# Expert rows kept as two 16-bit planes and turned by a transposing DMA, in a fused attention and expert kernel

## The chip, the cores and the metric

One core of a Trainium2 chip runs the whole program. The metric is the device time of one execution in microseconds; the kernel before takes 730.2 us (median of three runs, 729.65 to 731.32).

## The reference, cut to what matters

Three stages follow each other. The first is bucketed attention over 2 batches, 8 heads, 768 positions and 64 numbers per head; its result is laid out as 1536 token rows of 512 numbers. The second gives each token to the one expert of eight with the largest gate logit. The third is a gated feed-forward over all tokens.

```python
x = attn_out.transpose(0, 2, 1, 3).reshape(B * S, H * D)      # 1536 x 512
e_idx = np.argmax(x @ w_gate, axis=1)
for e in range(8):
    mask = e_idx == e
    h = np.maximum(x[mask] @ w1[e], 0.0)                       # 512 -> 1024
    out[mask] = gate_w[mask, None] * eom[mask, e, None] * (h @ w2[e])
return ((out @ w_a) * (out @ w_b)) @ w_out                     # 512 -> 1536 -> 512
```

## The kernel before, in words

All arithmetic is float32, most of it as a rounded high part and a rest (names ending in h and l), with three matmuls for one product. The order of every engine's instructions is the order of the program text, since a manual schedule is switched on.

**Attention.** A loop over 96 steps (16 heads of 6 query tiles, `h` and `t`) issues the scores of the next tile, the row minimum and the scale (`smax`, lines 164 and 165, on DVE), the exponential (line 173, on ACT), six TensorE transposes (line 186) and their copies out, and the product with v. Two heads later `o_out` (line 229) multiplies by an identity beside the gate weights; DVE writes the logits (line 248) and the head's 64 columns of `x_all` (line 249), and POOL adds the logits (line 251). POOL also makes the low parts of q and k (lines 116 to 119).

**Routing and scatter.** When batch 0 is done, `router` computes each token's slot, and `scat` sends each block of 128 rows of `x_all` by an indirect DMA from POOL to its rows in the DRAM table `xr`: 224 rows for each expert. Between two scatters POOL writes one column, `spare` (line 427). Batch 1's six scatters run after attention (259 to 267 us). For expert 0, `x0_load` fetches the rows of batch 0, and `x0_first`, `x0_hot` and `x0_add` put batch 1's rows in by matmuls, so that expert 0 can start ahead of the scatters.

**Experts.** A loop over 64 steps (expert `e`, slice `f` of 128 hidden columns). Each step issues `mm1(e, f)` (12 matmuls of 224 columns, lines 930 to 932), then `mm2` of the step before (8 matmuls, lines 970 and 971), then the split of the weights of coming steps (`w_split`: ACT line 484, DVE line 485), each of which issues the load of a slice four steps on (`w_load`, line 475, SP's queue). `x_load(e)` (line 910, SP's queue, ahead of the weight loads that follow it in the text) fetches an expert's rows, 2 times 128 rows of 2 KB. It waits for all scatters. `x_tpose` (line 912), at two steps of the expert before, turns half of them by four TensorE transposes (line 921); ACT and DVE split the result out of PSUM (lines 924 and 925). At the stage's start POOL clears `y_h`, `y_l` and `y_w` by twelve writes (line 815); `y_store(0)` writes into them at step (1, 1).

**Third stage.** A hand-made order of side work (`todo_of`) is laid between the matmuls.

Of the kernel before, what the change touches and what calls it, by code (L numbers as in the profile page):

```python
# [20 lines left out]
S, D, NB, NH = 768, 64, 2, 8  # L21
NT = 6
N, DM, E, FF, F2 = 1536, 512, 8, 1024, 1536
C = 224
# [9 lines left out]
def attn_moe_kernel(ctx: ExitStack, tc: tile.TileContext, xin, cst, projd, wblk, wmoe, w2in, out):  # L34
# [19 lines left out]

    xr = dram.tile([E * C + N, DM], F32, name="xr")
    idtab = dram.tile([N, 2], F32, name="idtab")
# [15 lines left out]
    noff_i = const.tile([128, 24], I32, name="noff_i")  # L72
    x_all = big.tile([128, 12, DM], F32, name="x_all")
    sums = big.tile([128, 96, 2], F32, name="sums")
# [131 lines left out]
    def av_group(h, q, ks):  # L206
# [3 lines left out]
        for k in ks:  # L210
# [3 lines left out]
            )  # L214

    oT, rs = {}, {}

# [11 lines left out]
    def o_out(h, q=None):  # L229
        b, hh = divmod(h, NH)  # L230
        o, r = oT.pop((h, q)), rs.pop((h, q))
        p = ps_m.tile([128, 512], F32, tag="m", name="m")
        t0, nt = q or (0, NT)
        t = slice(b * 6 + t0, b * 6 + t0 + nt)
        lp = sm.tile([128, nt, 16], F32, tag=f"lp{nt}", name="lp", bufs=2) if hh else lg[:, t]
        xo = x_all[:, t, hh * 64:(hh + 1) * 64]
# [12 lines left out]
        DVE.tensor_tensor(out=xo, in0=ps[..., :64], in1=rr.to_broadcast(sh + [64]), op=ALU.mult)  # L249
        if hh:  # L250
            (DVE if hh >= NH - 2 else POOL).tensor_tensor(out=lg[:, t], in0=lg[:, t], in1=lp, op=ALU.add)

    def router(gi):
# [103 lines left out]
        def scat(k):  # L357
            return lambda: scatter(
                scat_x, out=xr, out_offset=bass.IndirectOffsetOnAxis(ap=pos_i[:, k:k + 1], axis=0), in_=x_all[:, k],
                in_offset=None,  # L360
            )
# [8 lines left out]
    def x_split(d, t0=6, n=6):  # L370
        if d not in XH:
            XH[d] = [tb.tile([128, 6, 128], F32R, tag="tb"[i] + "qk"[d % 2], name="xh") for i in range(2)]
        h, l = (a[:, t0 - 6:t0 - 6 + n] for a in XH[d])
        x = x_all[:, t0:t0 + n, d * 128:(d + 1) * 128]
# [5 lines left out]
    def x0_load():  # L380
        x0["g"] = xp.tile([128, 2, DM], F32, tag="x", name="x0")
        for c in range(2):
            after(nc.sync.dma_start(out=x0["g"][:, c], in_=xr[c * 128:(c + 1) * 128]), scat_x)

# [40 lines left out]
    def scatter(done, **kw):  # L425
        if done:
            POOL.memset(spare, 0.0)
        ins = POOL.indirect_dma_start(**kw).ins
        for other in done:
            tc.declare_no_dep(ins, other, reason="each scatter writes rows of its own")  # L430
        done.append(ins)

    def after(ins, done):
        ins = ins.ins
        for other in done:
            tc.add_manual_dep(ins, other.name, dep, reason="reads what all the scatters wrote")
# [99 lines left out]
    def chunk(e, col, rr, new, psum):  # L536
# [11 lines left out]
        DVE.tensor_copy(tf[:, 0:1], tk.bitcast(I32)[:, 0:1])  # L548
        DVE.tensor_scalar(out=xi, in0=tf[:, 0:1], scalar1=float(E * C), scalar2=None, op0=ALU.add)
        x = new("f_x", [128, DM])  # L550
        POOL.indirect_dma_start(out=x, out_offset=None, in_=xr, in_offset=bass.IndirectOffsetOnAxis(ap=xi, axis=0))
        DVE.tensor_tensor(out=tf[:, 1:2], in0=rr, in1=col[:, 0:1], op=ALU.is_ge)
# [49 lines left out]
    with tc.manual_schedule():  # L602
# [49 lines left out]
        def set_up(k):  # L652
# [11 lines left out]
            elif k == 5:  # L664
# [10 lines left out]
        L = NHD - 1  # L675
        acts = (x0_load, lambda: x_split(0), lambda: (w_split(0, 0, POOL), w_split(0, 1, POOL)), lambda: x_split(1), lambda: x_split(2),
                lambda: w_split(1, 0, POOL))
# [5 lines left out]
        for g in range(NG):  # L683
# [8 lines left out]
            if 2 * NT <= g < 2 * NT + (E * C + N) // 256:  # L692
                for i in (g - 2 * NT,):
                    nc.sync.dma_start(
                        out=xr[i * 256:(i + 1) * 256].rearrange("(p r) d -> p r d", p=128),
                        in_=zeros[0].unsqueeze(1).to_broadcast([128, 2, 512]),
                    )
# [61 lines left out]
            if h and h < L and t == 5 and K["avl"].count(5):  # L759
                o_evac(h - 1)  # L760
            side(2)
            for f in extra.get((h - L + 1, t), ()):
                f()
# [15 lines left out]
        x0_hot(POOL, 7)  # L779
        x0_hot(POOL, 8)  # L780
        for t in (6, 7, 8):
            x0_add(t)
# [4 lines left out]
        rb["s2p"]()  # L787
        x_split(3, 10, 2)
        x0_add(9)
        for t in (10, 11):  # L790
# [21 lines left out]
        y_w = yp.tile([128, 4, N + C], F32, name="y_w")  # L812
        for y in (y_h.bitcast(F32), y_l.bitcast(F32), y_w):
            for d in range(4):
                POOL.memset(y[:, d], 0.0)
        r2 = ctx_2.enter_context(tc.tile_pool(name="r2", bufs=2, reuse_waits="tile"))
# [6 lines left out]
        yt = ctx_m.enter_context(tc.tile_pool(name="yt", bufs=4, reuse_waits="tile"))  # L823
        px = ctx_m.enter_context(tc.tile_pool(name="px", bufs=1, space=PSUM, reuse_waits="tile"))
        py = ctx_m.enter_context(tc.tile_pool(name="py", bufs=5, space=PSUM, reuse_waits="tile"))
# [78 lines left out]
        XG, HT, Y = {}, {}, {}  # L904

        def x_load(e):
            XG[e] = [xg.tile([128, DM], F32, tag=f"xg{c}", name=f"xg{c}") for c in range(2)]
            for c in range(2):
                r = e * C + c * 128
                after(nc.sync.dma_start(out=XG[e][c], in_=xr[r:r + 128]), scat_x)  # L910

        def x_tpose(e, halves):
            if e not in XS:
                XS[e] = [xs.tile([128, 4, C], F32R, tag="x" + "hl"[i], name="x" + "hl"[i]) for i in range(2)]
            h, l = XS[e]
            p = {i: px.tile([128, 512], F32, tag="x", name="xt") for i in halves}
            for c in range(2):
                for i in halves:
                    for j in range(2):
                        d, o = 2 * i + j, j * 256 + c * 128  # L920
                        PE.transpose(p[i][:, o:o + 128], XG[e][c][:, d * 128:(d + 1) * 128], ident)
            for i in halves:
                src = p[i].rearrange("p (a b) -> p a b", a=2)[:, :, :C]
                ACT.activation(h[:, 2 * i:2 * i + 2], src, ACTF.Copy)
                DVE.tensor_tensor(
                    out=l[:, 2 * i:2 * i + 2], in0=src, in1=h.bitcast(F32)[:, 2 * i:2 * i + 2], op=ALU.subtract
                )

# [102 lines left out]
        for n, (e, f) in enumerate(steps):  # L1031
# [212 lines left out]
        def todo_of(c, f):  # L1244
# [7 lines left out]
            def put(k, g, *a):  # L1252
                m[k].append(lambda: g(*a))
# [11 lines left out]
            elif (c, f) == (1, 0):  # L1265
                conv(1, 2, 0, 1, 1, 2)
                for k, g in ((0, t[7]), (1, t[8]), (2, t[9]), (3, t[10]), (4, t[11]), (5, u[1])):
                    put(k, g)
                put(3, w2_c, 1)
                for k, nm in ((4, "22"), (5, "s4"), (6, "21")):  # L1270
                    put(k, part, 1, nm)
                put(6, cc_work)
            elif (c, f) == (0, 1):
                for k, g in ((1, u[2]), (2, u[3]), (5, u[4]), (6, u[6])):
                    put(k, g)
# [10 lines left out]
            elif c == 0:  # L1286
# [131 lines left out]
```

## Time and profile before

| what | value |
|---|---|
| median of three runs | 730.2 us |
| the profiled execution, its own time | 730.29 us |
| span in its profile | 728.5 us |
| TensorE clock granted, mean | 0.997 |
| busy PE / DVE / ACT / POOL | 98% / 76% / 61% / 32% of the span |
| attention and its tail | 0 to 260 us |
| experts | 260 to about 430 us |
| third stage | to the end |

Starts and lengths are in microseconds from the span's start. PE is the matmuls, PEld the weight loads that overlap them. The time of the execution is 1.8 us above its span: what lies around the span.

### The profile page before, as it was taken

How to read it: one execution, taken by the hardware profiler on the slowest of the kernel's cores; microseconds unless marked ns; L12 is line 12 of the kernel's file. 1: busy time of each engine (PE TensorE's matmuls, PEld its weight loads, DVE VectorE, ACT ScalarE, POOL GpSimd, SP SyncE). 2: the span in 40 equal slices, each digit the busy share in tenths (PEclk: the TensorE clock that was granted, in tenths of full speed). 3: DMA queues.
4: the chain of work that ended last, by engine and by line, in shares of the span. 5: the costliest groups of instructions: out<-in, count | busy, mean ns of one | idle time of the engine just before them, and what ended most of it. 6: DMA issues, size and time to landing. Idle time of an engine off the chain costs nothing.

```text
span 728.5 us, 13206 instructions
## 1 busy us (share of the span) xinstructions
PE 711.2 (98%) x4561; PEld 609.0 (84%) x4562; DVE 552.4 (76%) x1102; ACT 448.0 (61%) x962; POOL 233.6 (32%) x269
## 2 busy tenths in 40 slices
PE   8899999999999999999999999999999999999995
PEld 6566776676676689999999999889999999999994
DVE  6778877888786778778778778886887877777644
ACT  5887787777777547667778766566443453444320
POOL 4232333232633368112220003234222333223234
PEclk9999999999999999999999999999999999999998
DMA  6357351131311048778798641132111222122013
GB/s 229 133 187 277 114 178 59 59 116 61 113 38 63 15 141 281 218 194 237 230 271 253 211 128 58 31 115 86 59 58 59 87 65 81 46 71 59 1 57 120
DMA packets 42681, 88.48 MB, mean 121 GB/s; under 512 B 7328, under 2 KB 10736, under 8 KB 42608
## 3 DMA queue, kind: packets, MB, share of 16 engines
q1 hardware_dynamic: 39936, 81.07, 36.0%
q0 software_dynamic: 2304, 6.31, 2.3%
q8 instruction: 38, 0.62, 0.4%
q14 instruction: 35, 0.29, 0.1%
q10 hardware_dynamic: 368, 0.20, 0.1%
HBM read 73.32 MB, written 13.12 MB: 119 GB/s over the span
## 4 chain that ended last, share of the span: by engine, by line
PE 82%; DVE 5%; issue 5%; ACT 4%; POOL 2%; DMA 1%; ACTq 0%; DVEq 0%; POOLq 0%; SPq 0%
PE tp L186 9%; PE av L201 8%; PE y L970 6%; PE s L158 4%; PE s L159 4%; PE h L932 4%; PE h L931 4%; PE h L930 4%; PE y L971 3%; PE abb L1186 3%; PE aba L1186 3%; PE abb L1188 3%; PE abb L1187 3%; PE aba L1188 3%; PE aba L1187 3%
## 5 line engine op out<-in xcount | busy, mean ns | idle before, releaser
L164 DVE TENSOR_REDUCE mm<-s 128x1 f32<-128x768 f32 x96 | 91.0, 948 | 25.2 <-PE s L159 24.5
L173 ACT ACTIVATE p<-s,sb 128x768 f32<-128x768 f32 x96 | 94.8, 988 | 22.3 <-DVE sb L165 21.7
L186 PEld LDWEIGHTS tp<-cs,p 128*128 128x128 f32 x576 | 64.2, 140 | 36.9 <-ACT p L173 23.5
L186 PE MATMUL tp<-cs,p 128*128 128x128 f32 x576 | 82.1, 278 | 4.9 <-ACT p L173 4.1
L485 DVE TENSOR_TENSOR wl<-wr,wh 128x512 fp32r<-128x512 f32 x125 | 81.4, 692 | 7.2 <-ACT wh L484 0.8
L190 ACT ACTIVATE pt<-tp 128x384 f32<-128x384 f32 x143 | 64.9, 487 | 32.6 <-PE tp L186 32.6
L901 POOL TENSOR_TENSOR pc<-t,pc 128x256 fp32r<-128x256 f32 x38 | 32.3, 854 | 156.5 <-ACT pc L900 141.9
L970 PE MATMUL y<-hl,wh 128*128 128x448 f32 x224 | 74.8, 377 | 0.4 <-DVE hl L944 0.3
L484 ACT ACTIVATE wh<-wr 128x512 fp32r<-128x512 f32 x128 | 73.5, 623 | 1.8 <-DMA wr<-wmoe 1.7
L158 PE MATMUL s<-tk,tq 76*128 76x384 f32 x192 | 73.0, 380 | 0.3 <-DVE tq L135 0.3
L930 PE MATMUL h<-xh,wh 128*128 128x224 f32 x256 | 71.4, 279 | 0.2 <-ACT xh L418 0.2
L931 PE MATMUL h<-xl,wh 128*128 128x224 f32 x256 | 70.2, 274 | 0.3 <-DVE xl L419 0.3
L932 PE MATMUL h<-xh,wl 128*128 128x224 f32 x256 | 70.4, 275 | 0.0
L201 PE MATMUL av<-pt,v 128*64 128x384 f32 x360 | 68.0, 499 | 0.2 <-DVE r L225 0.2
L159 PE MATMUL s<-bk,bq 128*128 128x384 f32 x192 | 65.1, 339 | 0.0
L971 PE MATMUL y<-hl,wl 128*128 128x224 f32 x224 | 59.5, 266 | 0.0
L1076 ACT ACTIVATE gh<-p 128x384 fp32r<-128x384 f32 x21 | 11.0, 526 | 64.4 <-DVE p L1205 64.4
L930 PEld LDWEIGHTS h<-xh,wh 128*128 128x128 f32 x256 | 48.9, 191 | 1.2 <-ACT xh L418 0.4
L931 PEld LDWEIGHTS h<-xl,wh 128*128 128x128 f32 x256 | 49.1, 192 | 0.5 <-DVE xl L419 0.5
L201 PEld LDWEIGHTS av<-pt,v 128*64 128x64 f32 x360 | 21.9, 136 | 32.8 <-issue 24.5
L932 PEld LDWEIGHTS h<-xh,wl 128*128 128x128 f32 x256 | 49.1, 192 | 0.0
L851 ACT ACTIVATE x<-r 128x512 uint8<-128x512 uint8 x36 | 28.5, 791 | 33.2 <-DVE x L848 33.2
(258 smaller groups left out, 1940.6 us busy)
## 6 DMA issues: line engine op xcount, KB each, us to landing
wr<-wmoe SPq DMA_DIRECT2D x128, 256.0 KB
r<-w2in SPq DMA_DIRECT2D x36, 512.0 KB
x<-xin SPq DMA_DIRECT2D x30, 384.0 KB
xr<-zero SPq DMA_DIRECT2D x13, 512.0 KB
xg<-xr SPq DMA_DIRECT2D x14, 256.0 KB
v<-xin SPq DMA_DIRECT2D x16, 192.0 KB
wb<-wblk SPq DMA_DIRECT2D x1, 640.0 KB
x<-xin SPq DMA_DIRECT2D x3, 192.0 KB
```

The lines of the kernel that those rows point to most:

```text
L158: PE.matmul(p[:, c, :384], T[h, 0][:76, qs], T[h, 1][:76, sl], start=True, stop=False)
L159: PE.matmul(p[:, c, :384], B[h, 0][:, qs], B[h, 1][:, sl], start=False, stop=True)
L164: DVE.tensor_reduce(out=m[:, 1:2], in_=st[g][:, :, :384], axis=AX.XY, op=ALU.min)
L173: ACT.activation(p.rearrange("p (c n) -> p c n", c=2), st.pop(g)[:, :, :384], ACTF.Exp, scale=scl.pop(g), bias=nbs.pop(g), accum_out=sums[ ...
L186: PE.transpose(ps[:, j * 128:(j + 1) * 128], pt_[g][:, k * 128:(k + 1) * 128], ident)
L201: PE.matmul(av[h][c * 64:(c + 1) * 64, :384], v, PT[h][:, k, c * 384:(c + 1) * 384], start=(k == 0), stop=(k == NT - 1), skip_group_check= ...
L485: eng.tensor_tensor(out=l, in0=r, in1=h.bitcast(F32), op=ALU.subtract)
L930: PE.matmul(ps, wh, xh, start=first, stop=False)
L931: PE.matmul(ps, wh, xl, start=False, stop=False)
L932: PE.matmul(ps, wl, xh, start=False, stop=last)
L970: PE.matmul(p, wh[:, w], hl, start=(f == 0), stop=False, skip_group_check=True)
L971: PE.matmul(p[:, 0], wl[:, w], hl[:, 0], start=False, stop=(f == 7), skip_group_check=True)
```

## The change

`xr` becomes a table of 32-bit words whose rows hold two planes: 512 low halves of the float32 numbers, then 512 high halves, each of 16 bits. Batch 0's heads go through a small tile `xf`, and POOL writes their halves into `x_q` (`to_planes`); batch 1's stay as float32 in `x_b` for the matmuls of expert 0, and POOL writes their halves later (`late_planes`). `x_load` becomes one DMA that turns 224 rows of 1024 16-bit numbers into eight blocks of 128 partitions; POOL joins the halves (`x_join`), and ACT and DVE split them from SBUF (`x_parts`). The TensorE transposes of experts 1 to 7 and their PSUM bank are gone. The column write between scatters becomes a no-operation. Eight of the twelve clearing writes move behind expert 1's join, and a few pieces of side work of the third stage change their slots.

```diff
+    def halves(ap):
+        return ap.bitcast(U16).rearrange("p t (n a) -> p t a n", a=2)
+    def to_planes(t0, nt, hh, src):
+        o = x_q.bitcast(U16).rearrange("p t (a n) -> p t a n", a=2)[:, t0:t0 + nt, :, hh * 64:(hh + 1) * 64]
+        POOL.tensor_copy(o, src)
+    def late_planes(hh, t0=0, nt=6):
+        to_planes(t0, nt, hh, halves(x_b)[:, t0:t0 + nt, :, hh * 64:(hh + 1) * 64])
...
         if hh:
             (DVE if hh >= NH - 2 else POOL).tensor_tensor(out=lg[:, t], in0=lg[:, t], in1=lp, op=ALU.add)
+        if not b:
+            to_planes(0, 6, hh, halves(xf))
+        elif NH + 3 <= h < L:
+            late_planes(hh)
...
+    def x0_join():
         x0["g"] = xp.tile([128, 2, DM], F32, tag="x", name="x0")
+        q = x0.pop("q").bitcast(U16).rearrange("p c (a n) -> p c a n", a=2)
         for c in range(2):
-            after(nc.sync.dma_start(out=x0["g"][:, c], in_=xr[c * 128:(c + 1) * 128]), scat_x)
+            POOL.tensor_copy(halves(x0["g"])[:, c], q[:, c])
...
-            POOL.memset(spare, 0.0)
+            POOL.nop()
...
+            if h == L - 2 and t > 2:
+                late_planes(t - 3)
...
         x0_hot(POOL, 8)
+        late_planes(NH - 1, 0, 4)
...
         x_split(3, 10, 2)
+        late_planes(NH - 1, 4, 2)
...
+        y_clear(y_h.bitcast(F32))
...
         def x_load(e):
-            XG[e] = [xg.tile([128, DM], F32, tag=f"xg{c}", name=f"xg{c}") for c in range(2)]
-            for c in range(2):
-                r = e * C + c * 128
-                after(nc.sync.dma_start(out=XG[e][c], in_=xr[r:r + 128]), scat_x)
+            XG[e] = xg.tile([128, 8, C], U16, tag="xg", name="xg")
+            after(nc.sync.dma_start(out=XG[e], in_=x_rows[e * C:(e + 1) * C], transpose=True), scat_x)
+        def x_join(e):
+            XI[e] = xg.tile([128, 4, C], F32, tag="xi", name="xi", bufs=1)
+            POOL.tensor_copy(
+                XI[e].bitcast(U16).rearrange("p d (n a) -> p a d n", a=2), XG.pop(e).rearrange("p (a d) n -> p a d n", a=2)
+            )
+        def x_parts(e, i):
+            h, l = (x[:, 2 * i:2 * i + 2] for x in XS[e])
+            src = XI[e][:, 2 * i:2 * i + 2]
+            ACT.activation(h, src, ACTF.Copy)
+            DVE.tensor_tensor(out=l, in0=src, in1=h.bitcast(F32), op=ALU.subtract)
...
-            if f in (5 if e == 0 else 4, 6) and e + 1 < E:
-                x_tpose(e + 1, (f // 2 - 2,))
+            if e + 1 < E:
+                if f == (3 if e else 5):
+                    x_join(e + 1)
+                for i in range(2):
+                    if f == ((4, 6) if e else (6, 7))[i]:
+                        x_parts(e + 1, i)
+            if (e, f) == (0, 5):
+                y_clear(y_l.bitcast(F32), y_w)
...
-                put(6, cc_work)
-                for k, g in ((1, u[2]), (2, u[3]), (5, u[4]), (6, u[6])):
+                for k, g in ((0, u[1]), (1, u[2]), (2, u[3]), (4, cc_work), (5, u[4]), (6, u[6])):
...
-                    for k, at in ((0, 4), (1, 4), (2, 5)):
+                    for k, at in ((0, 3), (1, 6), (2, 6)) if f == 2 else ((0, 4), (1, 4), (2, 5)):
```

## Rows read from the trace of the kernel before

**Rows 1.** Page, span and busy time of each engine.

```profile
span 728.5 us, 13206 instructions
PE 711.2 (98%) x4561; PEld 609.0 (84%) x4562; DVE 552.4 (76%) x1102; ACT 448.0 (61%) x962; POOL 233.6 (32%) x269
```

**Rows 2.** Stretches of the expert stage: busy of each engine, clock, DMA share, GB/s.

```profile
269.00:281.00 12.00, 11.67 (x88) 11.19 (x89) 10.11 (x31) 7.95 (x20) 12.00 (x8) 1.00 0.86 279
281.00:302.00 21.00, 21.00 (x162) 20.41 (x161) 17.33 (x41) 15.30 (x38) 9.33 (x10) 1.00 0.79 232
```

**Rows 3.** Groups by line, the transposes of expert rows and their split.

```profile
L921 PE MATMUL xt<-cs,xg 128*128 128x128 f32 x56 | 8.4, 273 | 0.0
...
L925 DVE TENSOR_TENSOR xl<-xt,xh 128x448 fp32r<-128x448 f32 x14 | 8.7, 622 | 0.6
...
L924 ACT ACTIVATE xh<-xt 128x448 fp32r<-128x448 f32 x14 | 7.6, 543 | 3.2 <-PE xt L921 3.2
```

**Rows 4.** Timeline of PE: first matmul of four steps, one transpose group (start, length).

```profile
276.54 0.35 PE L930 MATMUL h<-xh,wh 128*128 128x224 f32 x1
...
279.23 0.60 PE L921 MATMUL xt<-cs,xg 128*128 128x128 f32 x4
279.58 0.35 PE L930 MATMUL h<-xh,wh 128*128 128x224 f32 x1
...
282.27 0.28 PE L930 MATMUL h<-xh,wh 128*128 128x224 f32 x1
...
284.88 0.28 PE L930 MATMUL h<-xh,wh 128*128 128x224 f32 x1
```

**Rows 5.** Timeline of SP's queue, then ACT, then DVE, 268 to 277 us.

```profile
268.96 0.80 SPq L910 DMA_DIRECT2D xg<-xr  x2
269.87 11.43 SPq L475 DMA_DIRECT2D wr<-wmoe  x14
...
274.73 1.30 ACT L484 ACTIVATE wh<-wr 128x512 fp32r<-128x512 f32 x2 [1.72 <-DMA wr<-wmoe]
...
275.39 1.36 DVE L485 TENSOR_TENSOR wl<-wr,wh 128x512 fp32r<-128x512 f32 x2 [0.85 <-ACT wh L484]
```

**Rows 6.** Page, DMA queues: packets, MB, share of 16 engines' span.

```profile
q1 hardware_dynamic: 39936, 81.07, 36.0%
...
q10 hardware_dynamic: 368, 0.20, 0.1%
```

**Rows 7.** Timeline of DVE in step (0, 7), and PE in the step after.

```profile
281.59 0.39 DVE L944 SCALAR_TENSOR_TENSOR hl<-h,hl 128x224 fp32r<-128x224 f32 x1
282.11 1.29 DVE L485 TENSOR_TENSOR wl<-wr,wh 128x512 fp32r<-128x512 f32 x2
...
283.05 0.27 PE L931 MATMUL h<-xl,wh 128*128 128x224 f32 x1
```

**Rows 8.** Timeline of all engines in one attention head, 80 to 85 us.

```profile
80.17 0.82 POOL L119 CAST bk<-tk 64x768 fp32r<-64x768 f32 x1
80.44 0.56 DVE L165 SCALAR_TENSOR_TENSOR sb<-mm 128x2 f32<-128x2 f32 x1
...
81.31 0.39 POOL L251 TENSOR_TENSOR lg<-lg,lp 128x96 f32<-128x96 f32 x1 [0.33 <-DVE lp L248]
...
82.70 0.16 DVE L165 SCALAR_TENSOR_TENSOR sb<-mm 128x2 f32<-128x2 f32 x1
...
82.98 0.99 ACT L173 ACTIVATE p<-s,sb 128x768 f32<-128x768 f32 x1 [0.54 <-DVE sb L165]
...
84.23 0.74 PEld L186 LDWEIGHTS tp<-cs,p 128*128 128x128 f32 x6
```

**Rows 9.** Timeline of POOL: tail of attention, between two scatters, clearing writes.

```profile
255.38 0.73 POOL L376 TENSOR_TENSOR xh<-x_all,xh 128x256 fp32r<-128x256 f32 x1 [0.37 <-ACT xh L375]
...
260.57 0.12 POOL L427 MEMSET spare<- 128x1 f32 x1
...
281.08 6.11 POOL L815 MEMSET y_w<- 128x1760 f32 x4
```

More of the change, by code (lines that the diff above doesn't have):

```diff
@@ L12 @@
 U32 = mybir.dt.uint32
+U16 = mybir.dt.uint16
 U8 = mybir.dt.uint8
@@ L53, in attn_moe_kernel @@
     ident = cs[:, C_ID:C_ID + 128]
-    xr = dram.tile([E * C + N, DM], F32, name="xr")
+    xr = dram.tile([E * C + N, DM], U32, name="xr")
     idtab = dram.tile([N, 2], F32, name="idtab")
@@ L72, in attn_moe_kernel @@
     noff_i = const.tile([128, 24], I32, name="noff_i")
-    x_all = big.tile([128, 12, DM], F32, name="x_all")
+    x_b = big.tile([128, 6, DM], F32, name="x_b")
+    x_q = big.tile([128, 6, DM], U32, name="x_q")
     sums = big.tile([128, 96, 2], F32, name="sums")
@@ L235, in o_out @@
         lp = sm.tile([128, nt, 16], F32, tag=f"lp{nt}", name="lp", bufs=2) if hh else lg[:, t]
-        xo = x_all[:, t, hh * 64:(hh + 1) * 64]
+        if b:
+            xo = x_b[:, t0:t0 + nt, hh * 64:(hh + 1) * 64]
+        else:
+            xf = xo = sm.tile([128, 6, 64], F32, tag="xf", name="xf", bufs=2)
         if q is None:
@@ L358, in scat @@
             return lambda: scatter(
-                scat_x, out=xr, out_offset=bass.IndirectOffsetOnAxis(ap=pos_i[:, k:k + 1], axis=0), in_=x_all[:, k],
+                scat_x, out=xr, out_offset=bass.IndirectOffsetOnAxis(ap=pos_i[:, k:k + 1], axis=0), in_=x_q[:, k % 6],
                 in_offset=None,
@@ L373, in x_split @@
         h, l = (a[:, t0 - 6:t0 - 6 + n] for a in XH[d])
-        x = x_all[:, t0:t0 + n, d * 128:(d + 1) * 128]
+        x = x_b[:, t0 - 6:t0 - 6 + n, d * 128:(d + 1) * 128]
         ACT.activation(h, x, ACTF.Copy)
@@ L380, in x0_load @@
     def x0_load():
+        x0["q"] = xp.tile([128, 2, DM], U32, tag="x", name="x0q")
+        for c in range(2):
+            after(nc.sync.dma_start(out=x0["q"][:, c], in_=xr[c * 128:(c + 1) * 128]), scat_x)
+    def x0_join():
         x0["g"] = xp.tile([128, 2, DM], F32, tag="x", name="x0")
+        q = x0.pop("q").bitcast(U16).rearrange("p c (a n) -> p c a n", a=2)
         for c in range(2):
-            after(nc.sync.dma_start(out=x0["g"][:, c], in_=xr[c * 128:(c + 1) * 128]), scat_x)
+            POOL.tensor_copy(halves(x0["g"])[:, c], q[:, c])
     def x0_first(lo, hi):
@@ L549, in chunk @@
         DVE.tensor_scalar(out=xi, in0=tf[:, 0:1], scalar1=float(E * C), scalar2=None, op0=ALU.add)
+        xq = new("f_xq", [128, DM], U32)
+        POOL.indirect_dma_start(out=xq, out_offset=None, in_=xr, in_offset=bass.IndirectOffsetOnAxis(ap=xi, axis=0))
         x = new("f_x", [128, DM])
-        POOL.indirect_dma_start(out=x, out_offset=None, in_=xr, in_offset=bass.IndirectOffsetOnAxis(ap=xi, axis=0))
+        DVE.tensor_copy(
+            x.bitcast(U16).rearrange("p (n a) -> p a n", a=2), xq.bitcast(U16).rearrange("p (a n) -> p a n", a=2)
+        )
         DVE.tensor_tensor(out=tf[:, 1:2], in0=rr, in1=col[:, 0:1], op=ALU.is_ge)
@@ L675, in attn_moe_kernel @@
         L = NHD - 1
-        acts = (x0_load, lambda: x_split(0), lambda: (w_split(0, 0, POOL), w_split(0, 1, POOL)), lambda: x_split(1), lambda: x_split(2),
+        acts = (x0_load, lambda: x_split(0), lambda: (x0_join(), w_split(0, 0, POOL), w_split(0, 1, POOL)), lambda: x_split(1), lambda: x_split(2),
                 lambda: w_split(1, 0, POOL))
@@ L695, in attn_moe_kernel @@
                         out=xr[i * 256:(i + 1) * 256].rearrange("(p r) d -> p r d", p=128),
-                        in_=zeros[0].unsqueeze(1).to_broadcast([128, 2, 512]),
+                        in_=zeros[0].bitcast(U32).unsqueeze(1).to_broadcast([128, 2, 512]),
                     )
@@ L812, in attn_moe_kernel, with y_clear @@
         y_w = yp.tile([128, 4, N + C], F32, name="y_w")
-        for y in (y_h.bitcast(F32), y_l.bitcast(F32), y_w):
-            for d in range(4):
-                POOL.memset(y[:, d], 0.0)
+        def y_clear(*ys):
+            for y in ys:
+                for d in range(4):
+                    POOL.memset(y[:, d], 0.0)
+        y_clear(y_h.bitcast(F32))
         r2 = ctx_2.enter_context(tc.tile_pool(name="r2", bufs=2, reuse_waits="tile"))
@@ L823, in attn_moe_kernel @@
         yt = ctx_m.enter_context(tc.tile_pool(name="yt", bufs=4, reuse_waits="tile"))
-        px = ctx_m.enter_context(tc.tile_pool(name="px", bufs=1, space=PSUM, reuse_waits="tile"))
         py = ctx_m.enter_context(tc.tile_pool(name="py", bufs=5, space=PSUM, reuse_waits="tile"))
@@ L904, in attn_moe_kernel @@
         XG, HT, Y = {}, {}, {}
+        XI = {}
+        x_rows = xr.bitcast(U16)
         def x_load(e):
-            XG[e] = [xg.tile([128, DM], F32, tag=f"xg{c}", name=f"xg{c}") for c in range(2)]
-            for c in range(2):
-                r = e * C + c * 128
-                after(nc.sync.dma_start(out=XG[e][c], in_=xr[r:r + 128]), scat_x)
-        def x_tpose(e, halves):
-            if e not in XS:
[L914 to L927, printed above, removed]
+            XG[e] = xg.tile([128, 8, C], U16, tag="xg", name="xg")
[4 more added lines that the diff above has]
+                XI[e].bitcast(U16).rearrange("p d (n a) -> p a d n", a=2), XG.pop(e).rearrange("p (a d) n -> p a d n", a=2)
+            )
+        def x_parts(e, i):
+            if e not in XS:
+                XS[e] = [xs.tile([128, 4, C], F32R, tag="x" + "hl"[k], name="x" + "hl"[k]) for k in range(2)]
+            h, l = (x[:, 2 * i:2 * i + 2] for x in XS[e])
+            src = XI[e][:, 2 * i:2 * i + 2]
+            ACT.activation(h, src, ACTF.Copy)
+            DVE.tensor_tensor(out=l, in0=src, in1=h.bitcast(F32), op=ALU.subtract)
         def mm3(ps, wh, wl, xh, xl, first, last):
@@ L1266, in todo_of @@
                 conv(1, 2, 0, 1, 1, 2)
-                for k, g in ((0, t[7]), (1, t[8]), (2, t[9]), (3, t[10]), (4, t[11]), (5, u[1])):
+                for k, g in ((0, t[7]), (1, t[8]), (2, t[9]), (3, t[10]), (4, t[11])):
                     put(k, g)
```

## The prediction

> **What bounds the kernel now.** I read the page's busy times first, then stretches of the expert stage, then the groups of the lines that go, then timelines around each place that the change touches. PE is busy for 98% of the span, and its idle time is 17.3 us in all [rows 1]; so the reader is to look for matmul time that goes, and for waits that could open. In the expert stage PE shows no idle at all from 281 to 302 us, at full clock, while DVE works 17.3 of 21 us and ACT 15.3 [rows 2]. From 269 to 281 us PE idles 0.33 us, and the DMA engines are 86% busy [rows 2]: expert 0 is the one place where loads are close to deciding.
>
> **What goes: the transposes.** Their busy sum is 8.4 us for 56 [rows 3], but overlap of neighbours makes that no price. Steps give it: from 276.54 to 279.58, with one group of four, 3.04 us; from 279.58 to 282.27, with one more, 2.69, since the group at 279.23 already lies in the first; without one, 282.27 to 284.88, 2.61 us [rows 4]. The group costs 3.04 - 2.61 = 0.43 us where it stands alone. Seven experts times two groups are 14: 14 x 0.43 = **6.0 us off PE**, and as PE has no idle there, all of it comes back if no wait opens. The splits stay: DVE's 622 ns for 448 numbers out of PSUM [rows 3] against 1.36 / 2 = 0.68 us for 512 from SBUF [rows 5], 0.60 for 448. Equal, so nothing.
>
> **What is added: expert 1's load.** SP waits at 268.96 us for the last scatter, issues two plain loads, and only then the weight loads behind them [rows 5]. ACT waits 1.72 us until 274.73 for the first of these; DVE's half of that split ends at 275.39 + 0.68 = 276.07, and the matmul that reads it starts at 276.54 [rows 4, 5]. With the transposes ahead of it gone it would start at 276.11. The margin is nothing, so a load that holds the queue longer than the two plain ones stalls PE by the difference. The plain ones are 256 rows of 2 KB: 36.0% of 16 x 728.5 us over 39936 packets is 105 ns each at 2030 bytes [rows 1, 6]; 256 / 16 x 0.105 = 1.7 us. The transposing one spreads each row over eight blocks of 128 numbers, so its runs are 256 bytes: 224 x 8 = 1792, or 112 for each engine. No row shows a transposing DMA. If only bytes count, 256 / 2030 x 105 = 13 ns and 1.5 us; if a run costs what a 2 KB packet costs, 11.8 us. The nearest row by size is the queue with 543 bytes a packet: 0.1% of the engines' span over 368 is 32 ns [rows 6], and 112 x 0.032 = 3.6 us. I take that. The stall is 3.6 - 1.7 = 1.9 us, less what no-operations give: six scatters stand in a chain, a column write takes 0.12 us [rows 9], five of them at most 0.6, at least nothing, half taken. **+1.6 us**, ends 0 and 9.8. Later experts load eight steps ahead, and weights four steps (10.4 us) ahead of need, so 3.6 us is hidden there; were it over 10, not.
>
> [...]
>
> **Added: the join, and the later split.** Expert 1's second split now stands at step (0, 7), behind both weight splits. DVE's pair there ends at 282.11 + 1.29 = 283.40 [rows 7]; with 0.62 more it is 284.02, while the eighth matmul of the next step, which reads that half, starts at 283.05 [rows 7]. PE waits **+1.0 us** once (0 to 1.5). For experts 2 to 7 the splits stay at steps 4 and 6: nothing. A join copies 1792 numbers; at POOL's CAST, 0.82 us for 768 [rows 8], it takes 1.9 us. Nothing is queued behind it that is urgent. But while POOL copies, DVE's operations on two SBUF operands wait: the scale at 80.44 took 0.56 us and ended with the CAST, against 0.16 at 82.70 [rows 8]. The waiting split then holds DVE for up to 1.9 us; DVE has 3.7 us idle in an expert [rows 2] and the low part of h is ready at 281.98 [rows 7], 1.6 us ahead of its matmul, which comes twelve matmuls of 0.11 us after 282.27 [rows 4, 7], so I take nothing. That cover ends at a join of about 3.7 us. The clearing writes that move take 8 x 1.53 us [rows 9] behind the join, until about 290 instead of 281.08 + 6.11 = 287.2; `y_store(0)` asks for them at the end of step (1, 1), 284.88 + 2.61 = 287.5 [rows 4], and for `y_w` last. ACT may wait 0 to 1.5 us; h's slack covers it: nothing.
>
> **Added in attention.** Eight heads of batch 0 get a POOL copy of 768 numbers right after the logits' addition, which ends at 81.70; at 0.82 us it ends at 82.52, before the next scale at 82.70 [rows 8]. Nothing, then, by 0.18 us. Dearer per number is POOL's subtraction, 0.73 us for 256 [rows 9], 2.2 us for 768: the scale would wait 1.2 us, the exponential (82.98 to 83.97) would move past the weight load at 84.23 that needs it [rows 8], and PE would lose 1.2 - 0.26 = 0.9 us a head. The late copies of batch 1 and expert 0's join fall into POOL's idle time (it is busy for 32% [rows 1]), and what stands behind them in its queue (the first weight splits, the x splits) is read by PE only after attention. In the tail, 512 numbers (0.55 us) go in front of POOL's subtraction at 255.38 [rows 9]; its result is read only behind a further group of eight matmuls, but DVE's small two-operand steps wait for both: **+0.3 us** (0 to 0.7). The third stage only swaps slots of DVE work under a busy PE: nothing (0.5 either way).
>
> **Sum.** -6.0 + 1.6 + 1.0 + 0.3 = -3.1 us. The profiled execution took 730.3 us, 1.8 above its span and as good as the median of 730.2: **727.2 us**. From no change a measurement can tell about 0.2%, 1.5 us. With every stall at its low end the sum is -6.0, with half a microsecond from the third stage 723.8; with the load at 6 us it is -0.7 and 729.6. That is the forecast's own range; chance 0.60, of it 0.54 faster by over 0.2% and 0.06 within.
>
> **Rivals.** *The load is late* (slower). Place: the weight loads behind it in SP's queue at 270 us. With 105 ns a run it takes 11.8 us, the stall is 11.8 - 1.7 - 0.3 = 9.8, the sum +5.1 and the time **735.4 us**. It cancels the gain from a load of 3.6 + 3.1 = 6.7 us on. For it: the empty margin [rows 4, 5] and runs an eighth as long as a plain row. Against: small packets cost clearly less than large ones [rows 6]. Chance 0.20, of it 0.18 slower, 0.02 within. [...]
>
> [...] A copy between CAST and subtraction per number, 1.5 us, loses about 0.45 us in ten heads (eight, and heads 11 and 12): 4.5 us, **731.7 us**. It starts to cost at 1.26 us a copy. For it: the wait in [rows 8] and a margin of 0.18 us; against: a copy has one operand, as the CAST has. Chance 0.13: 0.07 within, 0.04 slower, 0.02 faster.
>
> *The transposes' time does not come back*: DVE, 83% busy in the stage [rows 2], sets the pace once PE has less. Then only the added terms remain less a part: about **730 us**, chance 0.07, within. Against it: DVE would still idle 3 us an expert. A small gain is in it: 0.02 of that faster.
>
> Together: faster 0.58, within 0.20, slower 0.22. The range leaves out about 0.2: from 723.8, below which only unlooked-for gains lie, to 736, just past the late load.
>
> **What would show it.** Right: no L921 on PE, steps of 2.61 us throughout experts 1 to 7, the expert stage 3 to 5 us shorter; one ACT wait for weights near 274 us longer by about 2 us, one PE wait at step (1, 0) on DVE's split; copies near 0.8 us and joins near 1.9. Wrong: steps above 2.7 us with waits on DMA in later experts, exponentials that wait on a scale stretched past 0.7 us at each head, or a SP queue held by the load's issue.

## The result, and the profile after

The changed kernel takes **736.83 us** (median of 4 runs, 735.29 to 738.25) against 730.03 us for the kernel before in the same session: ratio 1.0091, 95% interval 1.0078 to 1.0104. Slower by 6.8 us, where 3 us less was forecast; it lies above the range too. The profiled execution took 735.29 us, 1.8 us more than its span. Of all executions below one, of the run in which POOL only clears, took 1388.79 us and is left out of that run's ratio.

The page's span and busy times, which answer to [rows 1]:

```profile
span 733.5 us, 13070 instructions
PE 707.1 (96%) x4505; PEld 603.9 (82%) x4506; DVE 567.8 (77%) x1102; ACT 447.4 (61%) x962; POOL 260.1 (35%) x262
```

56 matmuls have gone, and with them 4 us of PE's busy time, but PE now idles 733.5 - 707.1 = 26.4 us where it idled 17.3. DVE has the same 1102 instructions and 15.4 us more busy time: something makes them longer. The same two stretches as in [rows 2]:

```profile
269.00:281.00 12.00, 9.61 (x69) 8.81 (x68) 9.25 (x23) 6.94 (x18) 10.83 (x7) 1.00 0.80 240
281.00:302.00 21.00, 17.94 (x121) 16.89 (x121) 17.07 (x41) 12.56 (x33) 13.55 (x10) 0.92 0.69 207
```

PE had no idle in the second stretch before; now 3.1 us, and the granted clock averages 0.92. The list of PE's waits (total us, how many, the longest) says for whom; shown are those that have no counterpart of their size in the kernel before, where h's low part cost 0.3 us in all:

```profile
PE y L1005 <- DVE hl L979: 6.5, 5, 2.5
...
PE h L967 <- DVE wl L511: 1.5, 1, 1.5
...
PE tp L188 <- DVE r L239: 1.1, 1, 1.1
...
PE h L966 <- DVE xl L962: 0.5, 1, 0.5
```

These four are all on DVE. Where they lie comes from PE's timeline, by the distance between the first matmuls of successive steps. Steps (1, 1) to (7, 1) take 2.61 to 2.68 us, as forecast, but four: (1, 3) takes 6.17 and (1, 4) 3.44, (4, 3) 4.33, (6, 3) 4.57. Step (1, 3) in the timelines of POOL, DVE and PE, in that order (the last three lines are the first matmuls of (1, 3), (1, 4) and (1, 5)):

```profile
292.39 1.26 POOL L454 DMA_INDIRECT idtab<-tokc,cpos_i  x1 [0.15 <-issue]
293.65 2.21 POOL L952 COPY xi<-xg 128x1792 uint16<-128x1792 uint16 x1
...
291.51 1.28 DVE L511 TENSOR_TENSOR wl<-wr,wh 128x512 fp32r<-128x512 f32 x2
292.71 3.96 DVE L1030 TENSOR_TENSOR y_l<-yt,y_h 128x224 f32 x4
296.60 0.38 DVE L979 SCALAR_TENSOR_TENSOR hl<-h,hl 128x224 fp32r<-128x224 f32 x1
...
297.03 0.48 PE L1005 MATMUL y<-hl,wh 128*128 128x448 f32 x1 [2.53 <-DVE hl L979]
...
293.00 0.27 PE L965 MATMUL h<-xh,wh 128*128 128x224 f32 x1
...
299.17 0.41 PE L965 MATMUL h<-xh,wh 128*128 128x224 f32 x1
...
302.61 0.28 PE L965 MATMUL h<-xh,wh 128*128 128x224 f32 x1
```

The join runs from 293.65 to 295.86. The four additions of `y_store`, 1.29 us in the kernel before, take 3.96, the third of them starting at 296.00, when the join has ended; h's low part is queued behind them and comes at 296.60, and PE waits 2.53 us for it. Then the clock, in stretches of 2 us with the columns of [rows 2]:

```profile
295.00:297.00 2.00, 0.00 (x0) 0.00 (x0) 2.00 (x5) 0.99 (x2) 0.87 (x1) 1.00 0.02 2
297.00:299.00 2.00, 1.97 (x8) 1.82 (x9) 2.00 (x4) 0.00 (x0) 0.00 (x0) 0.62 0.12 16
299.00:301.00 2.00, 2.00 (x11) 2.00 (x10) 0.68 (x2) 0.00 (x0) 0.00 (x0) 0.53 0.98 320
301.00:303.00 2.00, 2.00 (x17) 1.93 (x16) 0.89 (x2) 1.40 (x4) 0.41 (x2) 1.00 0.56 193
```

Behind the stretch in which PE did nothing the granted clock is 0.62 and 0.53 in two stretches of 2 us, and 1.00 in the one after them; the first matmul of (1, 4) takes 0.41 us where that of (1, 3) took 0.27. That is why (1, 4), which waits for nothing, takes 3.44 us, and why (1, 3) takes 1.03 us more than a plain step and its wait.

Where the time went, by stage of the profiled executions. "Attention" runs from the first row maximum to the first matmul of step (0, 0); steps (0, 0) to (0, 2) take 7.2 us in both kernels. A stretch of steps runs to the first matmul of the step after it. The time ahead of attention differs from execution to execution (9.8 to 11.0 us); it is the last term.

| us | before | changed | difference |
|---|---|---|---|
| attention and tail | 249.2 | 250.9 | +1.7 |
| steps (0, 3) to (1, 0) | 17.4 | 19.9 | +2.4 |
| steps (1, 1) to (7, 6) | 147.8 | 150.6 | +2.8 |
| from (7, 7) on, third stage | 295.8 | 295.2 | -0.7 |
| ahead of attention | 11.0 | 9.8 | -1.2 |

They sum to the spans' 5.0 us.

### The profile page after: what moved, and what is told of

Read it like the earlier page. It is cut to its first block, busy times and chain, and to the rows that moved or that the text cites. A ratio compares the mean times of both kernels' runs of the same rounds, so it can differ in the third digit from the quotient of the medians.

```text
span 733.5 us, 13070 instructions
## 1 busy us (share of the span) xinstructions
PE 707.1 (96%) x4505; PEld 603.9 (82%) x4506; DVE 567.8 (77%) x1102; ACT 447.4 (61%) x962; POOL 260.1 (35%) x262
## 4 chain that ended last, share of the span: by engine, by line
PE 82%; DVE 5%; POOL 4%; ACT 3%; issue 2%; DMA 2%; ACTq 0%; SPq 0%; DVEq 0%; POOLq 0%
PE tp L188 9%; PE av L203 8%; PE y L1005 5%; PE s L160 4%; PE s L161 4%; PE aba L1227 4%; PE abb L1227 4%; PE abb L1229 3%; PE aba L1229 3%; PE abb L1228 3%; PE aba L1228 3%; PE q L1157 3%; PE q L1158 3%; PE q L1156 3%; PE h L967 3%; PE h L965 3%
## 5 line engine op out<-in xcount | busy, mean ns | idle before, releaser
L511 DVE TENSOR_TENSOR wl<-wr,wh 128x512 fp32r<-128x512 f32 x125 | 89.4, 755 | 6.1 <-ACT wh L510 1.3
L1005 PEld LDWEIGHTS y<-hl,wh 128*128 128x128 f32 x224 | 42.6, 190 | 10.6 <-DVE hl L979 7.5
```

The source lines that it names most:

```text
L511: eng.tensor_tensor(out=l, in0=r, in1=h.bitcast(F32), op=ALU.subtract)
L1005: PE.matmul(p, wh[:, w], hl, start=(f == 0), stop=False, skip_group_check=True)
```

## The experiments

The theory from these rows: a POOL copy that reads and writes SBUF keeps DVE's operations on two SBUF operands waiting until it ends; where a join or a late copy meets work on DVE for which PE waits, the time is lost. In the changed kernel's trace the four additions take 3.96 us for 1.29 beside the join at 293.65, while h's low part, which has one operand in PSUM, keeps its 0.39 us at 339.43, inside the join that runs from 338.91 to 341.19. The traces show the waiting and not what makes it; "the port" in the expectations is the author's word for this theory. Rivals: the transposing load, POOL's occupation as such, the two-byte copy wherever it is done. All ratios are to the kernel before, run beside the kernel.

**No join.** `x_join` makes no copy; the split reads one constant tile.

```diff
-            XI[e] = xg.tile(...); POOL.tensor_copy(XI[e]..., XG.pop(e)...)
+            XI[e] = xi0
+            XG.pop(e)
```

> The joins are left out (the split of experts 1 to 7 reads a constant tile instead of their rows); the transposing loads stay. Theory of the port: a join of 2.2 us on POOL keeps DVE's two-operand subtractions waiting, and where it meets y_store (steps (1, 1) and (4, 1)), two weight splits (step (6, 1)) or the first weight splits (step (0, 6)), PE waits. Without joins the steps that began with PE waits (6.17, 3.44, 4.33 and 4.57 us instead of 2.61, together 8.1) fall back to 2.61, and the step before (0, 7) loses its 1.5 us: 736.8 - 9 = about 728. Rival, the load: it is the transposing DMA that delays the weights behind it; then the time stays within 1.5 us of 736.8.

728.06 us (726.85 to 729.33), ratio 0.998, interval 0.9971 to 0.999. The joins cost (1.0091 - 0.998) x 730 = **8.1 us** (6.4 to 9.7 at the ends of the two intervals), and no step from (1, 1) on is long that isn't long before, too: (1, 1) to (7, 6) take 142.5 us, 5.3 less than before. The additions of `y_store` are back at 383 ns from the changed kernel's 575:

```profile
L1030 DVE TENSOR_TENSOR y_l<-yt,y_h 128x224 f32 x28 | 9.0, 383 | 0.0
```

**The join held.** Experts 2 to 7 join one step earlier, held until that step's low part of h is done, so that POOL starts at another point of DVE's work.

```diff
-                if f == (3 if e else 5):
+                if f == (2 if e else 5):
+                    if e:
+                        POOL.tensor_copy(spare, HT[e, f].bitcast(F32)[:, 1, 0:1])
                     x_join(e + 1)
```

> For experts 2 to 7 the join moves to step (e, 2) and is held on POOL until the low part of h of that step is there, so that it runs behind y_store. Theory of the port: the three long steps of experts 1, 4 and 6 go (-3.6, -1.7, -2.0) and with them the clock's dip after the longest (-0.8): 736.8 - 8.1 = 728.7 us; the joins still take 2.2 us each and DVE still waits for them, but PE does not. Rival, the load: 736 to 737. Rival, the join's own length is too much for DVE anywhere: below 2 us gained, new waits at step (e, 3).

731.85 us (729.3 to 733.92), ratio 1.0044, interval 1.0029 to 1.006. Steps (1, 3), (1, 4), (4, 3) and (6, 3) are at 2.61 to 2.72 us; new collisions lie at (6, 5), 3.76 us, and, smaller, at (2, 4) and (5, 4), 3.14 and 3.15 us. With the same copies, started elsewhere, 3.4 of the joins' 8.1 us come back by the ratios; in the profiled execution, the quickest of five that spread over 4.6 us, it was 6.0 us of span. Where a copy starts decides. What the four slower executions (granted clock 0.992 to 0.995 for 0.998) lost, no trace shows.

**The late copies apart.** Of the late copies of heads 8 to 10 two wait for DVE's latest scale.

```diff
             if h == L - 2 and t > 2:
+                if t > 3:
+                    POOL.tensor_copy(held, last[0])
                 late_planes(t - 3)
```

> The late copies of heads 8 to 10 no longer follow each other on POOL: the second and third wait for the scale of a later step. Theory of the port: the scale that took 1.73 us at 213.2 us goes back below 0.9, PE's wait of 1.1 us near 216 goes, -1.5 us: 735.3 us. If the port is not the cause, the wait stays and the time is 736.8 within 1 us.

737.16 us (736.13 to 737.5), ratio 1.0104, interval 1.0087 to 1.0121: no gain in the total, where 1.5 us was expected. In the trace the scale takes 1.09 us for 1.73, PE's wait 0.49 for 1.13, and attention and tail take 250.3 us for 250.9, so 0.6 us came back there, and the collisions of the joins took it again, (6, 3) with 5.62 us.

**A plain load.** The same bytes come by a plain DMA, contiguous in each partition; the join copies them into a spare tile, and the split reads a constant one.

```diff
-            after(nc.sync.dma_start(out=XG[e], in_=x_rows[...], transpose=True), scat_x)
+            after(nc.sync.dma_start(out=XG[e].rearrange(...), in_=src), scat_x)
```

> Each expert's load is a plain DMA of the same 458752 bytes (128 partitions of 3584 bytes), not turned; the join writes a spare tile and the split reads a constant one, so what experts 1 to 7 compute is left wrong. Theory of the port: the joins still collide, the time stays within 2 us of 736.8; only the wait for weights near 275 us gets shorter, by less than 1 us. Rival, the load: SP's issue falls from about 1.6-4.4 us to 0.4, the weights come sooner and the time falls to 730 or below.

736.92 us (735.95 to 738.34), ratio 1.01, interval 1.0083 to 1.0116: as the changed kernel. So the load is not what makes the changed kernel slower. But the total does not show that transposing is free, since here too a join decides at that place (PE waits 2.61 us for h's low part in step (0, 6)). SP's queue and ACT, in this run and then in the run without joins:

```profile
271.47 0.33 SPq L951 DMA_DIRECT2D xg<-xr  x1
...
275.98 0.63 ACT L510 ACTIVATE wh<-wr 128x512 fp32r<-128x512 f32 x1 [2.69 <-DMA wr<-wmoe]
```

```profile
270.19 1.59 SPq L950 DMA_TRANSPOSE xg<-xr  x1
...
276.43 1.30 ACT L510 ACTIVATE wh<-wr 128x512 fp32r<-128x512 f32 x2 [3.93 <-DMA wr<-wmoe]
...
277.11 0.37 PE L965 MATMUL h<-xh,wh 128*128 128x224 f32 x1 [1.19 <-ACT wh L510]
```

From the load's issue to the split of the first weights behind it are 4.5 us with this plain load (5.8 and 5.1 with the old ones, in the kernel before and in it with the slots alone), and 5.9 to 6.5 in the eight traces in which the transposing load stands there; without joins PE waits for these weights. In the changed kernel the seven loads hold SP for 1.5 to 4.5 us each, here for 0.33 to 0.42. The packets of expert 1's load take 2.25 us from the first to the last in the changed kernel (1792 of 256 bytes, 19 ns each) and 1.71 here. What a plain load would be worth in the total without joins was not measured.

**POOL busy, but reading nothing.** Each join is replaced by three clearing writes of a spare tile; the split reads a constant one.

```diff
-            POOL.tensor_copy(XI[e]..., XG.pop(e)...)
+            for _ in range(3):
+                POOL.memset(xj, 0.0)
```

> The seven joins are replaced by three POOL clearing writes each of a spare 128x896 tile (about 2.4 us of POOL in the same place, writing SBUF and reading none); the split reads a constant tile. Theory (a join that reads and writes SBUF keeps DVE's operations on two SBUF operands waiting, and that wait reaches PE at steps 6, 11, 35 and 51): nothing of the joins' 7 to 8 us is lost, about 728 us as without joins, steps 11, 35 and 51 at 2.61 us, the y_store adds at 1.3 us. Rival (any POOL work at that place costs, because what is queued behind it on POOL comes later, or because writes alone hold DVE too): 735 to 737 us with the same long steps as the changed kernel.

728.82 us (727.15 to 730.82), ratio 0.9987, interval 0.9973 to 1.0001, as without joins. POOL's timeline, then DVE's, in experts 1 and 6:

```profile
294.86 2.67 POOL L957 MEMSET xj<- 128x896 f32 x3
...
295.43 1.28 DVE L511 TENSOR_TENSOR wl<-wr,wh 128x512 fp32r<-128x512 f32 x2
```

```profile
397.25 2.67 POOL L957 MEMSET xj<- 128x896 f32 x3
...
398.38 1.29 DVE L1033 TENSOR_TENSOR y_l<-yt,y_h 128x224 f32 x4
```

While POOL clears for 2.67 us, DVE's split pair and its four additions, all with two SBUF operands, keep their 1.28 and 1.29 us. So it is not POOL's being busy, nor its writes, but a copy, which also reads: the four additions take 3.96 us beside a join and 1.29 beside clearing writes.

**Joins on ACT**, four pieces of 448 numbers at steps (e, 2) to (e, 5); for expert 1 two each at (0, 5) and (0, 6), with its splits there.

```diff
-            POOL.tensor_copy(XI[e]..., XG.pop(e)...)
+            ACT.copy(o[:, :, j], XG[e].rearrange("p (a d) n -> p a d n", a=2)[:, :, j])
```

> Each join is made by ACT, in four pieces of 448 16-bit numbers at four neighbouring steps, and not by POOL. Theory (the loss is POOL's copy against DVE): long steps 11, 35 and 51 go, about 728 us plus what ACT's added 4 x 0.6 us an expert costs at its busiest steps (0 to 2): 728 to 730 us. Rival (the loss is in the two-byte strided copy wherever it is done, ACT being 73% busy in this stage): ACT's weight halves come late and PE waits on them, 733 us or more.

728.34 us (727.52 to 730.17), ratio 0.9993, interval 0.9983 to 1.0003; (1, 1) to (7, 6) take 142.8 us. ACT's copy is no quicker (0.70 us for 448 numbers), but from (1, 1) on PE waits nowhere over 0.3 us. In expert 0 it does: ACT's copies and splits stand ahead of h there, and PE waits 1.66 us in step (0, 7). The loss is POOL's copy against DVE, not the two-byte copy.

**Besides, the last copies.** The tail's copies go to ACT; those of heads 8 to 10 stay on POOL, one at a time, each held until DVE's latest scale.

```diff
-            if h == L - 2 and t > 2:
-                late_planes(t - 3)
+            if h == L - 2 and t == 3:
+                late_planes(0)
+            if h == L - 1 and t < 2:
+                POOL.tensor_copy(held, last[0])
+                late_planes(1 + t)
...
-        late_planes(NH - 1, 0, 4)
+        late_planes(NH - 1, 0, 4, ACT.copy)
...
```

> As the run with the joins on ACT, and besides: the last head's planes of the second batch are copied by ACT in the tail, and those of heads 8 to 10 by POOL one at a time, each held until DVE's last scale is done. Theory (the late copies cost 1.5 us at attention's end and 0.4 in the tail): 1 to 2 us below the run with the joins on ACT, about 727 us, which is below the kernel before. Rival (those waits only move): the same as the run with the joins on ACT within 0.5 us.

727.88 us (726.44 to 729.84), ratio 0.9984, interval 0.9971 to 0.9996. Attention and tail take 249.3 us, as before the change. The step from the last run, 0.7 us by the ratios and 0.5 in medians, is within the intervals; in the traces attention and tail are 1.5 us shorter. What is left is expert 0's start, (0, 3) to (1, 0), 19.8 us against 17.4. PE's waits there, then stretches:

```profile
PE h L968 <- ACT wh L510: 1.5, 1, 1.5
```

```profile
274.00:276.00 2.00, 0.54 (x4) 0.30 (x2) 0.32 (x1) 0.95 (x2) 2.00 (x2) 1.00 1.05 376
276.00:278.00 2.00, 1.75 (x12) 1.58 (x11) 1.36 (x4) 1.20 (x4) 2.00 (x3) 0.78 1.05 388
278.00:280.00 2.00, 2.00 (x9) 1.87 (x9) 1.34 (x2) 1.97 (x4) 2.00 (x2) 0.50 1.05 372
```

The weights of (0, 6) are late, with the DMA engines full, and the clock goes to half again. That wait is there in each run with the transposing load whose execution has no other wait ahead of it in steps (0, 3) to (0, 5), at 0.8 to 1.5 us; it is in none of the traces with plain loads.

**The third stage's new slots alone**, in the kernel before:

```diff
             elif (c, f) == (0, 1):
-                for k, g in ((1, u[2]), (2, u[3]), (5, u[4]), (6, u[6])):
+                for k, g in ((0, u[1]), (1, u[2]), (2, u[3]), (4, cc_work), (5, u[4]), (6, u[6])):
...
-                    for k, at in ((0, 4), (1, 4), (2, 5)):
+                    for k, at in ((0, 3), (1, 6), (2, 6)) if f == 2 else ((0, 4), (1, 4), (2, 5)):
```

> The kernel before with the change's new slots of the third stage alone (no planes, no joins, the old transposes). Theory (the 1.0 us that the third stage gains in all kernels with the change comes from these slots): 1.0 us below the kernel before, ratio about 0.9986. Rival (it comes from the gathered row's extra copy or from what stands ahead): within 0.3 us of the kernel before.

728.19 us (727.25 to 729.14), ratio 0.9985, interval 0.9976 to 0.9995: 1.1 us (0.4 to 1.8) of gain that has nothing to do with planes.

**Expert 1's rows asked for later**, behind the weight loads of (0, 4) to (0, 6):

```diff
-        x_load(1)
         for n, (e, f) in enumerate(steps):
...
+            if (e, f) == (0, 2):
+                x_load(1)
```

> As the run with joins and last copies on ACT, but expert 1's rows are asked for at step (0,2) and not ahead of step (0,0), so that the weight loads of steps (0,4) to (0,6) no longer stand behind it in SP's queue. Theory (what is left of the loss is expert 0's start: weights come late behind the transposing load, PE waits 1.5 us, and the two steps after it run at about half the clock; steps (0,6) to (1,0) are 4.1 us longer than 2.61 each): the matmuls of steps (0,5) to (1,0) come at 2.6 to 3.0 us, 3 to 4 us saved, 724 to 725 us. Rival (the weight loads then share the DMA engines with the scatters, which end later, and expert 1's rows come late instead): 727 to 729 us, with PE waiting for the split of x at step (1,0).

(The 4.1 us named there are of steps (0, 5) to (1, 0).)

**726.03 us** (725.15 to 726.31), ratio 0.9949, interval 0.9936 to 0.9963: faster than both kernels, below the run that it builds on by 1.9 us in medians and 2.6 in ratios, where 3 to 4 was expected. SP's queue, then the stretch of [rows 2]:

```profile
243.44 28.00 SPq L501 DMA_DIRECT2D wr<-wmoe  x7
272.08 1.89 SPq L951 DMA_TRANSPOSE xg<-xr  x1
...
281.00:302.00 21.00, 20.32 (x151) 19.54 (x152) 18.03 (x45) 19.08 (x46) 12.10 (x11) 1.00 0.76 202
```

The weights no longer stand behind the request that waits for the scatters; ACT waits for no weights there, (0, 3) to (1, 0) take 18.0 us, and the clock stays at 1.00. ACT, 15.3 us busy in the second stretch before, now works 19.1 of 21: there is little room for more on it.

**The same move without the change**, in the kernel with the slots alone (plain loads, transposes kept), the same diff:

> The kernel before with the third stage's new slots and the later request for expert 1's rows (plain loads, transposes kept): what the same move is worth without the change. Theory (before has only some 0.3 us of waits and 0.9 us of longer steps there): 0 to 1 us below the run with the slots alone, about 727.7 us. Rival (expert 1's rows come too late for the transposes at step (0,5)): 1 us or more above it.

728.96 us (728.33 to 729.85), ratio 0.9992, interval 0.9983 to 1.0001: nothing gained, 0.8 us above the run with the slots alone in medians, between what the theory and the rival say. It fits the load's price: behind the plain loads PE waits for no weights, so there is nothing for the move to save. The two moves are worth something together only: planes, their copies well placed, and this move bring (0.9985 - 0.9949) x 729.5 = 2.6 us over the slots alone (2.2 in medians).

**Joins on POOL, in halves**, at (e, 2) and (e, 4), each held on h; late copies apart; two of `y_h`'s four clearing writes ahead of expert 1's join, the other two behind it.

```diff
+                for i in range(2):
+                    if e and f == (2, 4)[i]:
+                        POOL.tensor_copy(spare, HT[e, f].bitcast(F32)[:, 1, 0:1])
+                        x_join(e + 1, slice(2 * i, 2 * i + 2))
```

> POOL keeps the joins, but each of experts 2 to 7 makes its own in two halves, at steps (e,2) and (e,4), each held until the step's h is done, so that neither meets DVE's long pairs with more than about 1.1 us; the last copies of batch 1 are held too, and only half of one clearing write goes ahead of expert 1's join. Theory (the loss is the length of one copy against what DVE has to do in that step, so a copy of half the length falls into DVE's idle time): long steps 11, 35, 51 and 53 go, 728 to 730 us. Rival (DVE loses the time in any case, 16 us of POOL copies in all): 733 us or more.

728.1 us (727.19 to 728.97), ratio 0.9981, interval 0.9971 to 0.999. POOL's, then DVE's timeline:

```profile
294.93 1.70 POOL L956 COPY xi<-xg 128x896 uint16<-128x896 uint16 x1
...
295.77 1.94 DVE L511 TENSOR_TENSOR wl<-wr,wh 128x512 fp32r<-128x512 f32 x2
```

A half takes 1.70 us, more than half of 2.2, and a pair of DVE still stretches from 1.28 to 1.94; but (1, 1) to (7, 6) take 143.4 us, only 1.0 more than with no join. POOL's copies need not cost much: what decides is what they meet, and for how long.

## Why the prediction was wrong

**The transposes: right.** Without joins, steps (1, 1) to (7, 6) are 5.3 us shorter, which is 12 groups at 0.44; the two groups of expert 1 cannot be told from expert 0's waits. The splits, taken as equal, are: 616 ns for 622 [rows 3]:

```profile
L952 POOL COPY xi<-xg 128x1792 uint16<-128x1792 uint16 x7 | 16.2, 2317 | 3.8 <-DMA xg<-xr 3.8
L1030 DVE TENSOR_TENSOR y_l<-yt,y_h 128x224 f32 x28 | 14.4, 575 | 0.0
L962 DVE TENSOR_TENSOR xl<-xi,xh 128x448 fp32r<-128x448 f32 x14 | 8.6, 616 | 0.0
```

**The join: this term failed.** The text had the effect (DVE's operations on two SBUF operands wait while POOL copies: the scale's 0.56 us for 0.16 [rows 8], here 3.96 us for 1.29) and nearly the length (1.9 us; the mean is 2.3). It took "nothing", because "DVE has 3.7 us idle in an expert [rows 2] and the low part of h is ready at 281.98 [rows 7], 1.6 us ahead of its matmul", and gave the cover an end at 3.7 us. Neither is the cover at the place where the join runs. The idle time is a sum over eight steps, and the 1.6 us were read in step (0, 7), which has no `y_store`. At the turn from (e, 2) to (e, 3), where the join ran in experts 1 and 4, DVE makes the four additions of `y_store(e - 1)`, in the kernel before too, between a split pair and h's low part with no idle on either side, and PE reads that low part at once (DVE, then PE, of the kernel before):

```profile
288.66 1.28 DVE L485 TENSOR_TENSOR wl<-wr,wh 128x512 fp32r<-128x512 f32 x2
289.86 1.29 DVE L995 TENSOR_TENSOR y_l<-yt,y_h 128x224 f32 x4
291.07 0.38 DVE L944 SCALAR_TENSOR_TENSOR hl<-h,hl 128x224 fp32r<-128x224 f32 x1
...
291.51 0.47 PE L970 MATMUL y<-hl,wh 128*128 128x448 f32 x1
```

The cover there was 0.06 us, from 291.45 to 291.51, and a join of 2.2 us cost 2.53 us of PE's wait and 1.86 more by the clock: (1, 3) and (1, 4) are 3.56 and 0.83 us over 2.61. Additions of `y_store` and joins have nothing that keeps them apart: in experts 1 and 4 an identity scatter ended just ahead of the join and they met; in expert 6 the join, behind a subtraction of POOL's that ended at 402.11, met a split pair (3.86 us for 1.29); the joins at 320.57, 338.91 and 385.01 us met other pairs and PE waited for none of them. The four long steps are 8.1 us over 2.61 each. The price of all joins was 8.1 us, and alone it turns the sign.

**POOL's late copies: failed too.** They "fall into POOL's idle time", but the cover that counts was again DVE's. Three in a row held the scale that an exponential waits for; POOL, DVE, ACT and PE:

```profile
212.58 2.35 POOL L224 COPY x_q<-x_b 128x768 uint16<-128x768 uint16 x3
...
213.22 1.73 DVE L167 SCALAR_TENSOR_TENSOR sb<-mm 128x2 f32<-128x2 f32 x1
...
215.06 0.99 ACT L175 ACTIVATE p<-s,sb 128x768 f32<-128x768 f32 x1 [2.10 <-DVE sb L167]
...
216.20 0.93 PE L188 MATMUL tp<-cs,p 128*128 128x128 f32 x6 [1.13 <-DVE r L239]
```

The scale takes 1.73 us for 0.16. From the 85th to the 89th of the 96 row maxima it is 11.1 us for 9.7, and 9.7 again when the copies were held apart in the run with all last copies moved.

**The copies at each head: right.** They start at the end of the logits' addition and take 0.82 us, as the CAST does; from the first row maximum to the 85th attention took 202.4 us for 202.3. The rival of 731.7 us, dearer copies at each head for which the scale waits, stood at 0.13: DVE does wait for POOL's copies, but in another place.

**Expert 0's start: near in size, and by another wait.** The sum had -0.9 for two groups, +1.6 for the load and +1.0 for the late split, together +1.7; measured +2.4. As a rival with a stall of 9.8 us the load falls: its packets took 19 to 27 ns and not 105, and a plain one gave 736.92 us. As a term it was near: forecast were 3.6 us for the load and a stall of 1.9. The packets of expert 1's load took 2.25 us, its issue held SP for 1.59 us where the two plain ones took 0.80, and in the run without joins PE waits 1.19 us for ACT's half of the weights behind it and 0.24 more for DVE's. A part of that is not the load's: the scatters that hold it back end 0.7 us later, which the forecast did not have. In the changed kernel all this is hidden under a wait that the join opens, so there the sum came near by luck. The longest of the seven loads took 3.7 us from its first packet to its last. Expert 1's packets come near those of a plain load, 2.25 us for 1.71 in the run with the plain load; the issue on SP does not, 1.59 us for 0.33. The packets came as counted: 7 x 1792 - 14 x 128 = 10752 more on q1 than in [rows 6].

```profile
q1 hardware_dynamic: 50688, 80.61, 36.1%
```

What opened there was the join again (POOL, DVE, PE; the pair takes 2.81 us for 1.36), and the late split with 0.53 us where 1.0 was forecast:

```profile
276.22 2.21 POOL L952 COPY xi<-xg 128x1792 uint16<-128x1792 uint16 x1
...
276.71 2.81 DVE L511 TENSOR_TENSOR wl<-wr,wh 128x512 fp32r<-128x512 f32 x2 [1.30 <-ACT wh L510]
...
278.98 0.37 PE L967 MATMUL h<-xh,wl 128*128 128x224 f32 x1 [1.54 <-DVE wl L511]
...
285.81 0.37 PE L966 MATMUL h<-xl,wh 128*128 128x224 f32 x1 [0.53 <-DVE xl L962]
```

Where the join is gone, late weights and the late split (1.11 us there) still cost about as much (19.5 us without joins); asking for the rows later brings 1.8 of it back. Of the 0.7 us by which the scatters end later after the start of step (0, 0), 0.5 is there at the first of the six; the cause stays open. A part of every difference in this stretch is none of the change's: (0, 3) and (0, 4) take 3.0 and 3.1 us in the traced execution of the kernel before, and 2.61 each in that of the run with the slots alone, which differs only in the third stage.

**The small terms.** The tail took 37.4 us for 37.3, with 0.3 forecast. The no-operations gave nothing, where 0.3 us was taken: scatters start 1.26 to 1.50 us after each other, before 1.26 to 1.38. The clearing writes cost nothing, as forecast. The third stage was put at 0.5 us either way and gained 1.1 by its slots alone, 0.7 in the changed kernel's trace.

So the sum of -3.1 should have been, from what was measured afterwards: -5.3 for the transposes of experts 2 to 7, +8.1 for the joins, +1.7 in attention and tail, +2.1 at expert 0's start without its join (+3.0 against the run with the slots alone, where that stretch took 16.5 us without the change), -1.1 in the third stage: +5.5 to +6.4, against 6.8 measured (5.7 to 7.6). The 8.1 is the difference of the runs with and without joins, so the sum checks the other terms and not that one.

## What to carry to other kernels

A wait that is said to be covered must be laid against the timeline of the engine that will wait, at the step where it will happen; busy shares and the slack of a neighbouring step are no cover. Before copies go to POOL, list DVE's operations on two SBUF operands that can run in that time and what is queued behind them: here four such operations took 3.96 us for 1.29 beside a copy of 2.21 us. A copy that must be on POOL is made short and held on something that DVE has finished; a free-running queue meets the critical operation in some iterations and not in others.

## What the runs showed that was not expected

- The price of a wait of PE is not its length alone. After waits of 2.53 us (changed kernel) and 1.46 us (joins and last copies on ACT, at 274 us) the granted clock stood at 0.50 to 0.78 in the next stretches; after one of 1.71 us at 406 us in the changed kernel it stayed at 1.00, and after one of 1.70 us at the same place in the run with the late copies apart it fell to 0.53.
- The two-byte copy's time on POOL is not proportional to its numbers: a join of 1792 took 2.21 to 2.73 us, half a join of 896 took 1.70, and the copy of 768 that parts the planes 0.82. Cutting joins in two made them dearer (22.7 us in all for 16.2) and the kernel faster.
- Two moves that each gain nothing, or little, alone (planes with good covers 0.9984 with the slots' 0.9985 in it; a later request 0.9992 for 0.9985) gave 0.9949 together.
